# Attention and MLP on one core: softmax denominators of two groups at once on 64x32 tiles, with their inverse rows copied by DMA

## The chip, the cores and the metric

The kernel runs on one core of one Trainium2 chip. Times are device microseconds of one execution. Profiles are of single executions; their span is about 2 us shorter than the time. Engines: PE is TensorE (PEld its weight loads), ACT ScalarE, DVE VectorE, POOL GpSimd, SP SyncE.

## The reference

Eight batches, twelve heads, 448 positions, head dimension 64. q and k are normalized by their root mean square and scaled by a gain per channel; then softmax attention; then an MLP of 768 to 2048 to 768 on all 3584 tokens.

```python
q_n, k_n = rmsnorm(q, g_q), rmsnorm(k, g_k)
attn = softmax(q_n @ k_n.T / 8)            # per batch and head, 448 x 448
x = (attn @ v).transpose(0, 2, 1, 3).reshape(B * S, H * D)
h = x @ w_in
out = (max(h, 0) + alpha * min(h, 0)) @ w_out
```

## The kernel before

Heads go in 24 groups of four. TensorE runs a recorded sequence of bursts: each has two or three score tiles (128 x 896), then perhaps the denominators ("den") or the product with v ("av") of an earlier group, then units of the MLP of an earlier batch: a first-MLP unit ("up", tiles hT or hTa, 6 matmuls) or half a second-MLP unit ("down", tile op, 16 matmuls). Scores, denominators and products use 64x64 tiles of the array, the MLP the whole array.

The denominators are a product of the exponentials with ones, so that each sum comes out on all 64 rows that need it:

```python
def over_keys(name, y, weights):
    acc = psa.tile([128, 2, 512], FP32, name=name, tag="acc")
    ...
    for j in range(J):                     # J = 7
        for g in range(2):
            for par in range(2):           # four 64x64 tiles at once
                nc.tensor.matmul(out=acc[ds(64 * par, 64), g, :S],
                    lhsT=weights(g, par, j), rhs=e[ds(64 * g, 64), j, par, :], ...)

def den(y):
    rden[y] = over_keys("dn", y, lambda g, par, j: ones[ds(64 * g, 64), :])
def log(y):        # ScalarE: Ln out of PSUM
def invert(y):     # ScalarE: Exp(-x), in place; attv multiplies by it on VectorE
```

GpSimd squares q and k and scales them; SyncE transposes them by DMA; VectorE multiplies the transposed k by the gain, in place, fp16 in SBUF:

```python
def square(y, nm):   ...  nc.gpsimd.tensor_mul(out=sqf, in0=src, in1=src)      # sq
def scale(y, nm):    ...  nc.gpsimd.tensor_mul(out=..., in0=nat, in1=rr...)    # qs
def turn(y):
    if y >= TD:                            # groups 8 to 23
        t = qkT[y, "k"]...
        nc.vector.tensor_scalar(out=t, in0=t, scalar1=gain[:, 0:1], ...)       # kT<-kT,gain
        return
```

Every engine works through its own instructions in the recorded order.

## Time and profile before

The median is 453.33 us. The span of the profile is 451.6 us.

| engine | busy us | share of the span |
|---|---|---|
| TensorE | 426.9 | 95% |
| ScalarE | 290.0 | 64% |
| VectorE | 207.8 | 46% |
| GpSimd | 171.2 | 38% |

Average shares mix three stages, so the prediction below reads them stage by stage.

### The profile page before, as it was taken

To read this page: it belongs to the slowest core of one execution; us is meant where nothing else is said; L and a number is where in the kernel's file an instruction comes from. 1 tells how busy PE (TensorE), PEld (TensorE's weight loads), DVE (VectorE), ACT (ScalarE), POOL (GpSimd) and SP (SyncE) were. 2 spreads that over 40 slices of the span, in tenths; PEclk is the share of its full clock that TensorE was granted. 3 is DMA by queue.
4 is the path that set the end of the run, shared out by engine and by line. 5 is a ranking of instruction groups with operands and counts; after the bars stand their busy time and mean duration, and the time that the engine had idled before them with its cause. 6 is when DMAs were issued, how large, how long until landed. Compare 5 with 4: busy or idle time off the path is not lost.

```text
span 451.6 us, 9099 instructions
## 1 busy us (share of the span) xinstructions
PE 426.9 (95%) x3848; PEld 230.0 (51%) x3848; DVE 207.8 (46%) x297; ACT 290.0 (64%) x401; POOL 171.2 (38%) x125
## 2 busy tenths in 40 slices
PE   8768989899999999999999999999999999999996
PEld 3334544555445545455545545455555555455563
DVE  3655553635463544444563544444563343343421
ACT  4998789557875848558785848558785846423300
POOL 5779952751472350750572350750542000000000
PEclk9999999999999999999999999999999999999999
DMA  8999995484655642764664642764361510111122
GB/s 191 233 247 241 232 240 117 60 168 110 158 94 127 159 105 53 140 156 118 157 109 111 158 107 53 139 157 118 77 100 38 77 37 1 37 35 36 35 71 70
DMA packets 60009, 52.77 MB, mean 117 GB/s; under 512 B 32688, under 2 KB 56512, under 8 KB 59968
## 3 DMA queue, kind: packets, MB, share of 16 engines
q1 hardware_dynamic: 47424, 39.27, 36.9%
q0 software_dynamic: 11808, 11.81, 16.7%
q10 hardware_dynamic: 736, 1.11, 1.0%
q8 instruction: 30, 0.49, 0.5%
q14 instruction: 11, 0.09, 0.1%
HBM read 45.62 MB, written 11.01 MB: 125 GB/s over the span
## 4 chain that ended last, share of the span: by engine, by line
PE 79%; ACT 14%; DVE 4%; DMA 1%; issue 1%; SPq 0%; ACTq 0%
PE op L301 31%; PE hT L284 18%; PE hTa L284 9%; ACT expT L229 8%; PE sc L217 7%; PE av L240 5%; PE dn L240 5%; ACT ah L292 2%; PE opa L301 2%; ACT rden L255 2%; DVE gT L293 2%; ACT rden L260 1%; DMA nat<-in_k_dram 1%; PE tps L193 1%; DVE ss L141 1%
## 5 line engine op out<-in xcount | busy, mean ns | idle before, releaser
L229 ACT ACTIVATE expT<-sc,expb 128x896 f16<-128x896 f32 x168 | 157.6, 1008 | 18.9 <-PE sc L217 18.7
L301 PE MATMUL op<-w_out_sb,gT 128*128 128x384 f16 x848 | 145.9, 326 | 2.1 <-DVE gT L293 2.0
L158 POOL TENSOR_TENSOR qs<-nat,rr 128x896 f16<-128x896 f32 x44 | 78.3, 1799 | 177.7 <-issue 159.0
L284 PE MATMUL hT<-xT,w_in_sb 128*128 128x448 f16 x558 | 117.1, 353 | 2.7 <-DVE gT L293 2.6
L301 PEld LDWEIGHTS <-gT 128*128 128x128 f16 x896 | 84.6, 98 | 65.5 <-issue 12.3
L284 PEld LDWEIGHTS <-w_in_sb 128*128 128x128 f16 x768 | 73.7, 98 | 72.8 <-issue 8.5
L292 ACT ACTIVATE ah<-hT,cols 128x448 f16<-128x448 f32 x93 | 59.1, 636 | 59.5 <-PE hT L284 59.4
L293 DVE TENSOR_TENSOR gT<-hT,ah 128x448 f16<-128x448 f32 x93 | 58.0, 624 | 76.5 <-ACT ah L292 76.5
L135 POOL TENSOR_TENSOR sq<-nat 128x896 f32<-128x896 f32 x44 | 73.0, 1681 | 1.4 <-DMA nat<-in_q_dram 1.3
L313 DVE COPY osb<-op 128x384 f32<-128x384 f32 x53 | 29.5, 557 | 89.4 <-PE op L301 89.4
L217 PE MATMUL sc<-qT,kT 64*64 64x448 f16 x672 | 53.2, 359 | 9.5 <-ACT expT L229 6.0
L292 ACT ACTIVATE ah<-hTa,cols 128x448 f16<-128x448 f32 x35 | 22.2, 633 | 49.5 <-PE hTa L284 49.5
L141 DVE TENSOR_REDUCE ss<-sq 128x14 f32<-128x896 f32 x48 | 49.8, 1076 | 6.5 <-ACT sq L133 6.1
L284 PE MATMUL hTa<-xT,w_in_sb 128*128 128x448 f16 x210 | 45.4, 352 | 0.0
L217 PEld LDWEIGHTS <-kT 64*64 64x64 f16 x672 | 19.2, 104 | 39.1 <-issue 29.0
L240 PE MATMUL av<-expT,vt 64*64 64x448 f16 x672 | 36.0, 350 | 2.2 <-ACT rden L255 2.2
L293 DVE TENSOR_TENSOR gT<-hTa,ah 128x448 f16<-128x448 f32 x35 | 21.8, 623 | 31.3 <-ACT ah L292 31.3
L240 PE MATMUL dn<-expT,ones 64*64 64x448 f16 x672 | 35.9, 349 | 0.2 <-DVE gT L293 0.2
L268 DVE TENSOR_TENSOR xT<-av,rden 128x896 f16<-128x896 f32 x24 | 26.2, 1090 | 20.7 <-PE av L240 20.7
L240 PEld LDWEIGHTS <-vt 64*64 64x64 f16 x672 | 20.3, 107 | 14.3 <-issue 3.7
L240 PEld LDWEIGHTS <-ones 64*64 64x64 f16 x672 | 20.5, 107 | 11.9 <-issue 1.0
L260 ACT ACTIVATE rden<-rden 128x896 f32<-128x896 f32 x24 | 23.0, 957 | 0.6
(37 smaller groups left out, 134.0 us busy)
## 6 DMA issues: line engine op xcount, KB each, us to landing
out_dram<-osb SPq DMA_DIRECT2D x54, 192.0 KB, 2.7
nat<-in_q_dram SPq DMA_DIRECT2D x46, 224.0 KB, 6.1
nat<-in_k_dram SPq DMA_DIRECT2D x46, 224.0 KB, 6.9
vt<-in_v_dram POOLq DMA_DIRECT2D x16, 336.0 KB, 7.6
w_in_sb<-in_moe_w_in_dram POOLq DMA_DIRECT2D x4, 768.0 KB, 13.2
w_out_sb<-in_moe_w_out_dram POOLq DMA_DIRECT2D x4, 768.0 KB, 16.6
nat<-in_q_dram ACTq DMA_DIRECT2D x2, 224.0 KB, 4.6
nat<-in_k_dram ACTq DMA_DIRECT2D x2, 224.0 KB, 6.1
```

Of the source, the lines that this page charges most:

```text
L135: nc.gpsimd.tensor_mul(out=sqf, in0=src, in1=src)
L141: nc.vector.tensor_reduce(out=ss_t[y][:, "qk".index(nm)].rearrange("p h j -> p (h j)").unsqueeze(2), in_=sqs[y, nm], axis=AXIS_X, op=ALU.add,)
L158: eng.tensor_mul(out=t.rearrange("p j h d -> p h j d"), in0=nat[y, nm], in1=rr_t[y][:, "qk".index(nm)].unsqueeze(3).broadcast_to((128, 2, ...
L217: nc.tensor.matmul(out=sc[ds(64 * g, 64), par, :S].rearrange("p (j c) -> p j c", j=J), lhsT=kT[ds(64 * par, 64), j, g, :], rhs=qT[ds(64 * ...
L229: nc.scalar.activation(out=expT[y][:, j], in_=scs[y, j][:, :, :S], func=AF.Exp, scale=QK_SCALE, bias=expb[:, 0:1],)
L240: nc.tensor.matmul(out=acc[ds(64 * par, 64), g, :S], lhsT=weights(g, par, j), rhs=e[ds(64 * g, 64), j, par, :], start=(j == 0), stop=(j == ...
L260: nc.scalar.activation(out=r, in_=r, func=AF.Exp, scale=-1.0)
L284: nc.tensor.matmul(out=hT[:, :S], lhsT=w_in_sb[:, c, ts(ft, 128)], rhs=x[:, c, :], start=(c == order[0]), stop=(c == order[-1]),)
L292: nc.scalar.activation(out=ah, in_=hT[:, :S], func=AF.Copy, scale=alpha_sb[:, ft : ft + 1])
L293: nc.vector.tensor_max(out=gT[:, ft, ds((b & 1) * S, S)], in0=hT[:, :S], in1=ah)
L301: nc.tensor.matmul(out=op[:, :OH], lhsT=gT[:, ft, ts(t, 128)], rhs=w_out_sb[:, ft, ds(oh * OH, OH)], start=(ft == 0), stop=(ft == NF - 1),)
L313: nc.vector.tensor_copy(out=o[:, ds(oh * OH, OH)], in_=op[:, :OH])
```

## The change

From group 6 on the denominators of two groups are computed together. A 64x32 tile puts each sum on 32 rows only, so eight tiles run side by side in place of four. One Ln then serves two groups, and the Exp is written twice. Each inverse then has the right values in two bands of 32 rows and the other group's in the other two, which a DMA within SBUF overwrites. The rest makes room for that: a third buffer for the exponentials, "down" units kept for bursts with den or av, row sums a burst sooner, av two or three bursts behind its den. To fit, the squares have three buffers where they had four, and ah two where it had three.

```diff
+    def den(ys):
+        if len(ys) == 1: ...              # as before, groups 0 to 5
+        dn = psa.tile([128, 2, 512], FP32, name="dn2", tag="acc")
+        for j in range(J):
+            for par in range(2):
+                for n, y in enumerate(ys):
+                    for g in range(2):
+                        nc.tensor.matmul(
+                            out=dn[ds(64 * par + 32 * n, 32), g, :S],
+                            lhsT=ones[ds(64 * g, 64), :32],
+                            rhs=expT[y][ds(64 * g, 64), j, par, :], ...)
...
+        for y in ys:
+            nc.scalar.activation(out=rden[y], in_=r, func=AF.Exp, scale=-1.0)
+        if len(ys) == 2:
+            for n, y in enumerate(ys):
+                for c in range(2):
+                    nc.gpsimd.dma_start(
+                        out=rden[y][ds(64 * c + 32 * (1 - n), 32)],
+                        in_=rden[y][ds(64 * c + 32 * n, 32)],
+                    )
...
-                if old and (free or not ups):
+                if old and (not ups or free and (
+                    wide(n) or len(old) > sum(wide(c) for c in range(n, hi))
+                )):
...                                        # bursts, jobs, turns and spare banks
```

More of the change, by code (lines that the diff above doesn't have):

```diff
@@ L49 @@
     TD = min(8, NG)
+    PD = min(6, NG)
+    EB = 3
     cst = ctx.enter_context(tc.tile_pool(name="cst", bufs=1))
@@ L129, in square @@
         src = nat[y, nm].rearrange("p h j d -> p (h j d)")
-        sq = ld.tile([128, 2 * J, D], FP32, name="sq", tag="sq", bufs=4)
+        sq = ld.tile([128, 2 * J, D], FP32, name="sq", tag="sq", bufs=3)
         sqf = sq.rearrange("p n d -> p (n d)")
@@ L227, in soft @@
         if j == 0:
-            expT[y] = att.tile([128, J, 2, S], FP16, name="expT", tag="expT")
+            expT[y] = att.tile([128, J, 2, S], FP16, name="expT", tag="expT", bufs=EB)
         nc.scalar.activation(
@@ L247, in over_keys, with log, invert @@
         return acc
-    def den(y):
-        dn = over_keys("dn", y, lambda g, par, j: ones[ds(64 * g, 64), :])
-        rden[y] = dn
-    def log(y):
-        r = att.tile([128, 2, S], FP32, name="rden", tag="rden")
-        nc.scalar.activation(out=r, in_=rden[y][:, :, :S], func=AF.Ln)
-        rden[y] = r
-    def invert(y):
-        r = rden[y]
-        nc.scalar.activation(out=r, in_=r, func=AF.Exp, scale=-1.0)
+    def den(ys):
+        if len(ys) == 1:
+            rden[ys[0]] = over_keys(
+                "dn", ys[0], lambda g, par, j: ones[ds(64 * g, 64), :]
+            )
+            return
+        dn = psa.tile([128, 2, 512], FP32, name="dn2", tag="acc")
[6 more added lines that the diff above has]
+                            lhsT=ones[ds(64 * g, 64), :32],
+                            rhs=expT[y][ds(64 * g, 64), j, par, :],
+                            start=(j == 0),
+                            stop=(j == J - 1),
+                        )
+        for y in ys:
+            rden[y] = dn
+    def log(ys):
+        r = att.tile([128, 2, S], FP32, name="rden", tag="rden")
+        nc.scalar.activation(out=r, in_=rden[ys[-1]][:, :, :S], func=AF.Ln)
+        rden[ys[-1]] = r
+    def invert(ys):
+        r = rden[ys[-1]]
+        for y in ys[:-1]:
+            rden[y] = att.tile([128, 2, S], FP32, name="rden", tag="rden")
+        for y in ys:
+            nc.scalar.activation(out=rden[y], in_=r, func=AF.Exp, scale=-1.0)
[5 more added lines that the diff above has]
+                        in_=rden[y][ds(64 * c + 32 * n, 32)],
+                    )
     def attv(y):
@@ L290, in up @@
             )
-        ah = ffn.tile([128, S], FP16, name="ah", tag="ah", bufs=3)
+        ah = ffn.tile([128, S], FP16, name="ah", tag="ah", bufs=2)
         nc.scalar.activation(out=ah, in_=hT[:, :S], func=AF.Copy, scale=alpha_sb[:, ft : ft + 1])
@@ L335 @@
     bursts, dens, avs, first_in, last_in = [], {}, {}, {}, {}
+    den_at, av_at = {}, {}
     m = 0
     while m < NG * J or len(avs) < NG:
-        n = len(bursts)
-        if len(dens) > len(avs):
-            avs[n] = len(avs)
-        elif len(dens) < NG and last_in.get(len(dens), n) < n:
-            dens[n] = len(dens)
-        wide = n in dens and dens[n] >= G or n in avs and avs[n] >= G
-        count = min(3 if wide else 2, NG * J - m)
-        bursts.append([divmod(m + c, J) for c in range(count)])
-        for y, j in bursts[n]:
-            first_in.setdefault(y, n)
+        n, y, d = len(bursts), len(avs), len(den_at)
+        if y in den_at and n - den_at[y] >= (2 if y >= PD else 1):
+            avs[n] = y
+            av_at[y] = n
+        elif d < NG:
+            ys = [d] if d < PD else [d, d + 1]
+            if all(last_in.get(g, n) < n for g in ys):
+                dens[n] = ys
+                den_at.update((g, n) for g in ys)
+        three = n in dens and dens[n][0] >= G or n in avs and avs[n] >= G
+        tiles = []
+        while len(tiles) < (3 if three else 2) and m < NG * J:
+            g, j = divmod(m, J)
+            if j == 0 and g >= EB and not (
+                g - EB in av_at and (av_at[g - EB] < n or len(tiles) == 2)
+            ):
+                break
+            tiles.append((g, j))
+            first_in.setdefault(g, n)
             if j == J - 1:
-                last_in[y] = n
-        m += count
+                last_in[g] = n
+            m += 1
+        bursts.append(tiles)
     NB = len(bursts)
-    den_at = {y: n for n, y in dens.items()}
-    av_at = {y: n for n, y in avs.items()}
     prep, post, roots = {}, {}, {}
@@ L366 @@
     turns = {n: y for y, n in turn_at.items()}
-    jobs = {}
-    for y in range(G, NG):
-        early = y < G + 2
-        n = turn_at[y - 1] if early else max(d for d in dens if d <= turn_at[y] - 2)
-        at(n - (8 if early else 5), load_qk, y)
-        for nm in "qk":
-            (after if early else at)(n - 2, square, y, nm)
-            if early:
-                after(n, reduce, y, nm)
-            else:
-                jobs.setdefault(n, []).append((reduce, (y, nm)))
-        roots[n + 1] = y
-    for b in range(1, B):
-        at(av_at[G * b] - 4, load_v, b)
     UP, DOWN = 1.13, 2.6
@@ L402, in cost, with wide @@
         )
+    def wide(n):
+        return n in dens or n in avs
     first = av_at[G - 1]
+    begin = [av_at[G * b + G - 1] for b in range(B)]
+    for b in range(3, B - 1, 2):
+        begin[b] = max(begin[b], (begin[b - 1] + begin[b + 1]) // 2)
     gaps = [[] for _ in range(NB)]
     for b in range(B - 1):
-        lo, hi = av_at[G * b + G - 1], av_at[G * b + 2 * G - 1]
+        lo, hi = begin[b], begin[b + 1]
         ups, old, new = (list(u) for u in periods[b])
@@ L435 @@
     rest += [u[1:] for u in old + new]
+    jobs = {}
+    for y in range(G, NG):
+        early = y < G + 2
+        n = turn_at[y - 1] if early else turn_at[y] - 4
+        if not early:
+            for c in (4, 5, 3):
+                if turn_at[y] - c not in jobs and any(
+                    u[0] is down for u in gaps[turn_at[y] - c]
+                ):
+                    n = turn_at[y] - c
+                    break
+            while n in jobs:
+                n -= 1
+        at(n - (8 if early else 5), load_qk, y)
+        for nm in "qk":
+            (after if early else at)(n - 2, square, y, nm)
+            if early:
+                after(n, reduce, y, nm)
+            else:
+                jobs.setdefault(n, []).append((reduce, (y, nm)))
+        roots.setdefault(n + 1, []).append(y)
+    for b in range(1, B):
+        at(av_at[G * b] - 4, load_v, b)
     load_qk(0)
@@ L481 @@
         at(first - 2 + c, load_w_out, c)
-    roots[4] = 2
+    roots.setdefault(4, []).append(2)
     for n in range(NB):
@@ L507 @@
             attv(avs[n])
+        pair = n in dens and len(dens[n]) == 2
+        if pair:
+            log(dens[n])
         for t in tiles[2:]:
@@ L513 @@
             late = [(1, soft, t) for t in tiles[1:]]
-        if n in roots:
-            y = roots[n]
+        for y in roots.get(n, ()):
             root(y)
@@ L520 @@
                 turn_dma(y)
-        if n in dens and not lead:
+        if n in dens and not lead and not pair:
             log(dens[n])
@@ L526 @@
                 late = [(1, invert, (dens[n],))]
+        elif pair:
+            if gaps[n] and gaps[n][0][0] is down:
+                invert(dens[n])
+            else:
+                late = [(2, invert, (dens[n],))]
         done = 0
-        spare_at, clock = None, 0.0
+        spare_at, clock = [], 0.0
         for k, (f, a) in enumerate(gaps[n][:-1]):
             free = 2.3 if n in dens else 1.2 if n in avs else 0.1
-            if spare_at is None and clock >= free and not turns.get(n, TD) < TD:
-                spare_at = k
+            if clock >= free and not turns.get(n, TD) < TD and (
+                not spare_at or k - spare_at[-1] > 2
+            ):
+                spare_at.append(k)
             clock += DOWN if f is down else UP
         for k, (f, a) in enumerate(gaps[n]):
-            spare = k == spare_at
+            spare = k in spare_at
             if f is down:
@@ L545 @@
                     late = []
-            if k == 0 and n in turns:
+            if n in turns and k == (
+                0 if turns[n] >= TD else max(min(1, len(gaps[n]) - 2), 0)
+            ):
                 turn(turns[n])
@@ L551 @@
             g(*c)
-        if n < first and plain and n not in turns:
+        if n < den_at[G - 1] - 1 and plain and n not in turns:
             spin(4)
```

## The prediction

> **What bounds the kernel now.** I read first the windows view, cut where the chain of work changes hands (columns: length, then busy us of PE, PE weight loads, DVE, ACT, POOL, each with its instruction count, then clock, DMA share, GB/s).
>
> ```profile
> 0.00:92.00 92.00, 76.45 (x813) 39.51 (x814) 48.82 (x65) 72.90 (x101) 63.05 (x55) 1.00 0.96 198
> 92.00:375.00 283.00, 278.70 (x2558) 150.45 (x2556) 133.53 (x192) 196.77 (x273) 108.12 (x70) 1.00 0.52 111
> 375.00:451.60 76.60, 71.71 (x481) 40.06 (x478) 25.45 (x41) 20.29 (x30) 0.00 (x0) 0.99 0.16 42
> ```
>
> From 92 to 375 us TensorE works 278.70 of 283.00 us at full clock; every other engine has over 80 us free. Before 92 us ScalarE (72.90) rivals TensorE, and the last stretch is MLP work alone with a drain of the output. What TensorE still waits for after 92 us is little, by the view of waits cut to that stretch:
>
> ```profile
> PE hT L284 <- DVE gT L293: 2.4, 5, 0.9
> PE op L301 <- DVE gT L293: 2.0, 2, 1.0
> PE dn L240 <- DVE gT L293: 0.2, 1, 0.2
> ```
>
> So there a microsecond of TensorE work removed is a microsecond of time, if no new wait comes. I then read what one denominator costs, in the chain of work (start, us, what):
>
> ```profile
> 204.24 0.50 PE sc L217 x8
> 204.75 1.32 PE dn L240 x28
> 206.07 0.19 PE sc L217 x4
> 206.26 2.71 PE op L301 x16
> ```
>
> The single instructions behind this show four dn matmuls (four 64x64 tiles) starting 3.3 ns apart, and the next four 189 ns after the first: 7 steps of 189 ns = 1.32 us per group, 24 groups.
>
> They also show what a change of tile shape costs. Eight score matmuls followed by dn or av in the same shape take 0.402 us, by op or hT 0.505; six hT before scores take 1.228 us, before another unit 1.135; the first score step is 24 ns longer, the first op step behind scores 10. One visit to 64x64 and back is thus 0.103 + 0.093 + 0.024 + 0.010 = 0.23 us.
>
> ScalarE's rows, which decide where it may become the bound:
>
> ```profile
> L229 ACT ACTIVATE expT<-sc,expb 128x896 f16<-128x896 f32 x168 | 157.6, 1008 | 18.9 <-PE sc L217 18.7
> L292 ACT ACTIVATE ah<-hT,cols 128x448 f16<-128x448 f32 x93 | 59.1, 636 | 59.5 <-PE hT L284 59.4
> L260 ACT ACTIVATE rden<-rden 128x896 f32<-128x896 f32 x24 | 23.0, 957 | 0.6
> L255 ACT ACTIVATE rden<-dn 128x896 f32<-128x896 f32 x24 | 22.3, 929 | 1.3 <-PE dn L240 1.3
> ```
>
> **What the Trainium skill says.** "TensorEngine Tiling (Array Packing)", Tiling Modes, lists 64x32 as eight independent tiles, and says that changing the mode drains the engine. The trace agrees on the drain (the 0.23 us a visit); it has no 64x32 tile. "TensorE: Matmul & The Clock Gate", Part 3, gives concurrent tiles a span of one matmul plus about 4 ns per further tile, up to 16 tiles; the trace agrees for four (3.3 ns). "ScalarE: Activation LUTs", What ACT_TABLE_LOAD costs, prices an ACTIVATE by elements per lane, not by partitions; so one Ln over four 32-row bands costs what it costs today. The 0.93 us of 128x896 fits. "DMA: Bandwidth & Descriptors", Anatomy of one DMA, gives a fixed cost near 2 us; here small transfers land in 2.7 us (out_dram<-osb) to 3.4 (kT<-qs, a transpose).
>
> **The change part by part.** I took the order of instructions of both kernels and counted.
>
> 1. Denominators. Groups 6 to 23 (18 groups) go in 9 pairs of 56 matmuls. With all eight tiles at once a step is 189 + 4 x 3.3 = 202 ns at worst, more likely 189 with 13 ns once, so a pair takes about 1.34 us. Saved: 18 x 1.323 - 9 x 1.34 = 23.8 - 12.1 = 11.7 us of TensorE, all after 96 us, on the path.
>
> 2. Tile-shape changes. Bursts grow from 66 to 77, as a pair's two av come two and three bursts behind its den, and waiting for two groups makes bursts without den or av. Visits out of 128x128 go from 61 to 70: 9 x 0.23 = 2.1 us. A pair also changes 64x64 to 64x32 and back, 16 changes in the order; half a visit (0.115) each is my estimate: 1.8 us. Matmul counts of all other kinds are equal but for one idle filler of four in the opening.
> Net TensorE work: -11.7 + 2.1 + 1.8 = -7.8 us.
>
> 3. ScalarE. A pair needs one Ln and two Exp instead of two and two: 9 x 0.929 = 8.4 us less. It isn't the bound in the large stretch (196.77 of 283), so this buys nothing there by itself.
>
> 4. New waits on ScalarE by rearrangement. With den 6 put off to be paired with 7, bursts 21 to 24 hold two score tiles and 1, 2, 3, 3 first-MLP units, where the old burst 21 had a second-MLP unit (2.6 us of TensorE with no ScalarE work). Sums for bursts 19 to 26, from the rows above plus 0.55 us for each root (0.33 + 0.23): ScalarE 4.9 + 3.7 + 3.2 + 3.3 + 4.5 + 3.9 + 5.9 + 3.8 = 33.2 us. TensorE, with 1.13 us a unit, 2.6 a second-MLP unit, 0.6 a plain score visit: 2.1 + 6.6 + 1.7 + 2.9 + 4.0 + 4.0 + 5.0 + 2.9 = 29.2. A plain burst with two first-MLP units also puts its second exp behind the first unit's ah, so the next burst's second score tile waits some 0.5 us (score tiles have two buffers). I follow it burst by burst and get waits of 1.85, 0.3, 0.3, 1.0, 0.5, 0.55 us in bursts 21 to 31: 4.5 us. The old kernel loses 1.8 between 96 and 133 us (0.09, 0.86, 0.07, 0.77), which putting second-MLP units behind den is made to remove. Net +2.7. From burst 31 on, bursts have four or five units or a second-MLP unit, and TensorE's sum is larger again. The 1.0 us waits of op behind the last unit of a sequence (189 and 291 us) stay: the order is the same there.
>
> 5. The opening. Turning group 4 behind two units rather than one removes most of the 1.1 us wait at 64.6 us; dropping a filler of four brings 0.2 at most, as the Ln behind it also waits for the root before it (ends 41.22, Ln starts 41.43). Taken: -1.2.
>
> 6. The copies. 36 of 115 KB (32 x 896 x 4 bytes), 4.1 MB beside 52.8. GpSimd issues one in 0.5 to 0.7 us (rows 0.50, vt 0.68): 18 to 25 us more on an engine that works 108 of 283. Is a pair's inverse there in time? From the end of the denominators: Exp of both ready at about 3.7 and 4.7 us (first two exps, Ln, third exp, Exp, Exp), two issues 1.2 us, landing 3 us: 7.9 us for the first group. Its av ends, by the order, 0.3 + 2.6 + 0.6 + 2.3 + 0.4 + 1.3 = 7.5 us on for the first pair, 7.8 for the second, 10 to 11 for the others; and behind that av stands a second-MLP unit of 2.6 us that needs neither the product nor VectorE until its end. So nearly all is hidden. GpSimd waiting in order for the Exp delays the next squares and scales by some 6 us; for group 10 I find kT ready at about 22.0 us against its first score at 22.3. I allow 1 us for copies and turns together. Earlier row sums are there to make this fit.
>
> Sum: -7.8 + 2.7 - 1.2 + 1.0 = -5.3, and about -0.4 for other waits that the shorter bursts behind den lose: 453.3 - 5.7 = 447.6 us.
>
> **The rivals.**
> A. The eight tiles don't run at once: two moving streams per row of the array are shown in this trace, four aren't. Then a pair takes 2.65 us, nothing is saved, and the switches and waits stay: 453.3 + 3.9 + 1.5 = about 459. Against it: the skill's table of packed tiles. I give it 12%.
> B. The change of column width costs little (weights of seven tiles are loaded while the last streams), and the rearrangement removes the ScalarE waits rather than moving them: -11.7 + 2.1 + 0.5 - 1.8 - 1.2 = -12, about 441. For it: parts of the change look like answers to just such waits. Against: bursts 21 to 26 have more ScalarE work than TensorE work. 20%.
> C. The inverse copies are late (landing 6 us as the q and k loads, 6.1 and 6.9, when they share the 16 engines): VectorE then stands in order behind xT, gT comes late, the MLP banks fill. Two tight pairs would lose 2 to 3 us each, and delayed turns 1 us on each of several groups: 452 to 455. Against it: DMA share is 0.52 in that stretch. 10%.
>
> **Range and chances.** The remaining 58% lie within 2.5 us of 447.6. With the rivals' places, 8 in 10 is 442.0 to 455.0. Faster by over 2% means under 444.3, 3.3 us below my sum, which rival B and the edge of the middle give: 0.24. Slower by over 2% means over 462.4, past even rival A: 0.04. Within: 0.72.
>
> **What would show it.** The steps in turn: (1) eight dn2 matmuls starting within 30 ns and the next eight 190 to 200 ns later, a pair near 1.34 us in the chain; (2) the gap between scores and dn2 near 0.1 us; (3) half of the Ln gone from burst 25 on; (4) TensorE waiting for expT between 96 and 130 us, some 4 us in sum, and next to nothing later; (6) xT waiting for a rden copy at most at the first two pairs, copies landing in about 3 us. A dn2 step near 380 ns makes the prediction wrong by rival A; xT or kT waits for DMA throughout by rival C; no ScalarE waits in 96 to 130 us by rival B.

## More of the kernel before

One more view matters for what came, that of the instructions that write kT. Its columns are the shortest, median and longest duration in ns, then first and last start in us.

```profile
L179 DVE TENSOR_SCALAR kT<-kT,gain x16: 445/658/975, 112.9 to 362.9; 128x896 f16<-128x896 f16 x16
```

Sixteen products of kT with the gain take 0.45 to 0.98 us.

## The result

The changed kernel takes 463.48 us (463.47 to 464.16, four runs) against 453.6: the ratio is 1.0222, with a 95% interval of 1.0204 to 1.024, so slower. A ratio here is the mean time of one kernel's fast runs over that of the other's of the same rounds, so it is not quite the ratio of the medians.

The windows view of the changed kernel, with columns as in the prediction and the middle cut once more:

```profile
0.00:92.00 92.00, 76.07 (x802) 38.88 (x803) 45.92 (x63) 71.99 (x100) 60.04 (x52) 0.98 0.94 195
92.00:135.00 43.00, 36.01 (x327) 17.35 (x326) 24.41 (x28) 28.52 (x42) 21.68 (x17) 0.92 0.60 120
135.00:386.00 251.00, 241.47 (x2271) 122.28 (x2268) 122.91 (x167) 163.00 (x227) 104.26 (x88) 0.99 0.57 120
386.00:461.70 75.70, 71.05 (x450) 39.65 (x449) 25.48 (x41) 17.41 (x26) 1.97 (x4) 0.99 0.19 48
```

TensorE now idles 7.0 of 43 us right behind the opening and 9.5 of 251 after that, and its clock there is 0.92 and 0.99 where it was 1.00.

First, did the tiles do what they were to do? The timeline of TensorE around a pair (start, us, engine, line, what):

```profile
309.02 0.57 PE L219 MATMUL sc<-qT,kT 64*64 64x448 f16 x8
309.53 1.52 PE L263 MATMUL dn<-expT,ones 64*32 64x448 f16 x56
310.97 0.38 PE L219 MATMUL sc<-qT,kT 64*64 64x448 f16 x4
```

They did. From 309.53 to 310.97 it is 1.44 us for two groups, where one took 1.32. By the single instructions, eight matmuls start within 24 ns, the next eight 199 ns after the first, and the steps after that are 189 ns apart.

Then the waits of TensorE after 92 us (what waited, for what: us in total, times, longest):

```profile
PE hT L315 <- DVE gT L324: 6.2, 4, 5.2
PE sc L219 <- DVE kT L181: 5.9, 5, 3.8
PE sc L219 <- ACT expT L231: 3.5, 6, 1.4
```

The third line was predicted. The first two hold one wait of 5.2 us and one of 3.8, and these are new. The chain of work through the second one (start, us, what):

```profile
121.37 5.81 DVE kT L181
127.18 0.04 issue
127.22 0.59 PE sc L219 x4
127.81 5.23 PE op L332 x16
133.04 0.50 PE sc L219 x8
```

An instruction that took at most 0.98 us takes 5.81, and 16 op matmuls behind it take 5.23 us instead of 2.60. The view of kT's product, to be held against the row of the kernel before:

```profile
L181 DVE TENSOR_SCALAR kT<-kT,gain x16: 444/887/5798, 112.0 to 363.7; 128x896 f16<-128x896 f16 x16
```

What else ran then? The timeline of VectorE and of GpSimd in the same stretch:

```profile
121.37 5.80 DVE L181 TENSOR_SCALAR kT<-kT,gain 128x896 f16<-128x896 f16 x1
127.09 0.61 DVE L324 TENSOR_TENSOR gT<-hT,ah 128x448 f16<-128x448 f32 x1
```
```profile
118.23 2.06 POOL L288 DMA_DIRECT2D rden<-rden  x4 [5.83 <-ACT rden L283]
120.31 3.33 POOL L137 TENSOR_TENSOR sq<-nat 128x896 f32<-128x896 f32 x2
123.58 3.33 POOL L160 TENSOR_TENSOR qs<-nat,rr 128x896 f16<-128x896 f32 x2
```

GpSimd stood 5.83 us at the copies, for ScalarE's Exp. Released, it issued them and then ran two squares and two scales without a gap, from 120.31 to 126.91. VectorE's product began within that row and ended 0.26 us behind it. The same happens at 317.55 (5.80 us, again behind two squares and two scales); there gT stands behind it on VectorE and TensorE waits the 5.2 us.

Four findings make up the loss. The stall at 127 us costs 3.8 us and then 2.6 in which op runs at half speed; that at 324 us costs 5.2 and 1.3 (six hT matmuls in 2.40 us instead of 1.14): 12.9 us together. ("TensorE: Matmul & The Clock Gate", Part 1 of the Trainium skill, has the clock halve after an idle window of about 3.4 us. The window agrees, as the half-clock stretches of these traces, but for those cut off by their ends, last 3.41 or 6.83 us. But TensorE need not idle through all of it: it worked 0.80 us of the 3.42 us before the first halving and none before the second, and in before_useless_copies below a pause of 1.56 us was enough, with 1.70 us of work in the 3.41 us before.) A copy that landed late adds 1.3 and 0.7 at 159 to 161 us, and three smaller kT waits 1.4. That is some 16 us; the run without copies below keeps 2.2 us of kT waits, so about 14 of them would be the copies'.

My theory (called L in the expectations): a product on VectorE can't run while GpSimd works through a row of its own instructions, and the copies on GpSimd's queue put such a row where the product is due. The Trainium skill, "SBUF — State Buffer", Who interferes with whom, describes the first half: VectorE's `tensor_scalar` may use two ports, of which one pair is shared with GpSimd and lent to one of them exclusively. I hadn't looked that page up. In the same trace VectorE's other work is not held: all 128 gT products take 0.61 to 0.63 us, 53 of them while GpSimd works. No run here gave the product a form that leaves the shared ports alone, so that it is the ports rests on the page and on this timing. The rival (S): the new order of bursts itself is at fault, kT comes too late or VectorE is overfilled, and the copies are bystanders.

### The profile page after: what moved, and what is told of

Same layout as the page of the kernel before. It is cut to its first block, busy times and chain, and to the rows that moved or that the text cites. A ratio compares the mean times of both kernels' runs of the same rounds, so it can differ in the third digit from the quotient of the medians.

```text
span 461.7 us, 9170 instructions
## 1 busy us (share of the span) xinstructions
PE 424.6 (92%) x3844; PEld 218.2 (47%) x3844; DVE 218.7 (47%) x297; ACT 280.9 (61%) x392; POOL 188.0 (41%) x161
## 4 chain that ended last, share of the span: by engine, by line
PE 68%; ACT 17%; DVE 9%; DMA 3%; issue 2%; SPq 0%; POOL 0%; DVEq 0%; ACTq 0%
PE op L332 28%; PE hT L315 18%; ACT expT L231 9%; PE hTa L315 7%; PE sc L219 7%; PE av L242 5%; DVE kT L181 3%; ACT rden L283 3%; ACT ah L323 2%; PE opa L332 2%; DMA rden<-rden 2%; ACT rden L275 2%; DVE gT L324 2%; PE dn L263 2%; DVE ss L143 2%
## 5 line engine op out<-in xcount | busy, mean ns | idle before, releaser
L231 ACT ACTIVATE expT<-sc,expb 128x896 f16<-128x896 f32 x168 | 161.4, 1006 | 34.9 <-PE sc L219 34.7
L332 PE MATMUL op<-w_out_sb,gT 128*128 128x384 f16 x848 | 148.4, 330 | 0.0
L315 PE MATMUL hT<-xT,w_in_sb 128*128 128x448 f16 x588 | 124.5, 355 | 7.7 <-DVE gT L324 6.4
L323 ACT ACTIVATE ah<-hT,cols 128x448 f16<-128x448 f32 x98 | 62.1, 633 | 86.2 <-PE hT L315 80.8
L324 DVE TENSOR_TENSOR gT<-hT,ah 128x448 f16<-128x448 f32 x98 | 61.2, 624 | 82.5 <-ACT ah L323 82.2
L288 POOL DMA_DIRECT2D rden<-rden x36 | 18.3, 515 | 89.9 <-ACT rden L283 89.8
L315 PE MATMUL hTa<-xT,w_in_sb 128*128 128x448 f16 x180 | 38.9, 352 | 0.0
L323 ACT ACTIVATE ah<-hTa,cols 128x448 f16<-128x448 f32 x30 | 19.1, 636 | 24.9 <-PE hTa L315 24.9
L324 DVE TENSOR_TENSOR gT<-hTa,ah 128x448 f16<-128x448 f32 x30 | 18.7, 623 | 21.9 <-ACT ah L323 21.9
L181 DVE TENSOR_SCALAR kT<-kT,gain 128x896 f16<-128x896 f16 x16 | 22.1, 1380 | 0.0
```

The costliest lines, as they stand in the source:

```text
L231: nc.scalar.activation(out=expT[y][:, j], in_=scs[y, j][:, :, :S], func=AF.Exp, scale=QK_SCALE, bias=expb[:, 0:1],)
L315: nc.tensor.matmul(out=hT[:, :S], lhsT=w_in_sb[:, c, ts(ft, 128)], rhs=x[:, c, :], start=(c == order[0]), stop=(c == order[-1]),)
L323: nc.scalar.activation(out=ah, in_=hT[:, :S], func=AF.Copy, scale=alpha_sb[:, ft : ft + 1])
L324: nc.vector.tensor_max(out=gT[:, ft, ds((b & 1) * S, S)], in0=hT[:, :S], in1=ah)
L332: nc.tensor.matmul(out=op[:, :OH], lhsT=gT[:, ft, ts(t, 128)], rhs=w_out_sb[:, ft, ds(oh * OH, OH)], start=(ft == 0), stop=(ft == NF - 1),)
```

## The experiments

Each is one edit of the kernel that its expectation names, except sync_gain_pool, which changes the engine and the place of the product together. Ratios are to the kernel before in the same rounds, whose medians were 453.6 to 454.2 us.

**No copies.** The result is wrong (its relative error is 0.96).

```diff
-        if len(ys) == 2:
+        if False:
```

> The changed kernel without the 36 copies; the result is wrong on purpose. Theory L with its cause in GpSimd's order: 445 to 449 us, the time that the change would have without the copies' side effects, ScalarE waits of TensorE of some 6 us between 96 and 145 us left. Rival S: 456 to 463 us, as only the one xT wait (2 us) goes.

449.04 us, ratio 0.9889 (0.9856 to 0.9922). The waits of TensorE after 92 us:

```profile
PE sc L219 <- ACT expT L231: 3.5, 6, 1.4
PE sc L219 <- DVE kT L181: 2.2, 2, 1.4
PE hT L315 <- DVE gT L324: 1.3, 4, 0.4
```

Without 36 small DMAs the order of bursts is all the same, and 14.4 us are gone. S falls. The 3.5 us for expT are the price of the new order (I had expected some 6), and the longest kT product here is 2.24 us.

**Only the copies, in the kernel before.** The reverse: nothing of the change except useless copies by GpSimd.

```diff
         nc.scalar.activation(out=r, in_=r, func=AF.Exp, scale=-1.0)
+        if y >= 6 and y % 2:
+            for c in range(4):
+                nc.gpsimd.dma_start(
+                    out=spare_rows[ds(32 * c, 32)], in_=r[ds(32 * (c ^ 1), 32)])
```

> The kernel before plus, behind each odd group's inverse from group 7 on, four copies of 32 rows issued by GpSimd into a tile that nobody reads: only GpSimd's standing still at the Exp and its four issues are added. Theory L with its cause in GpSimd's order: squares are held back and reach kT's products in some bursts, at least one kT product over 3 us, 455 to 466 us. Rival (it takes the new order of bursts too): every kT product under 1.7 us, 453 to 454.5 us.

462.24 us, ratio 1.018 (1.0163 to 1.0197): clear of noise. The result is correct. The timelines of VectorE and GpSimd at the worst product:

```profile
227.69 4.94 DVE L180 TENSOR_SCALAR kT<-kT,gain 128x896 f16<-128x896 f16 x1
```
```profile
223.87 0.50 POOL L264 DMA_DIRECT2D spare_rows<-rden  x1
224.38 3.33 POOL L136 TENSOR_TENSOR sq<-nat 128x896 f32<-128x896 f32 x2
227.66 3.33 POOL L159 TENSOR_TENSOR qs<-nat,rr 128x896 f16<-128x896 f32 x2
230.93 1.36 POOL L111 DMA_DIRECT2D vt<-in_v_dram  x2
```

In the kernel before, at this place:

```profile
227.88 0.97 DVE L179 TENSOR_SCALAR kT<-kT,gain 128x896 f16<-128x896 f16 x1
```
```profile
226.91 3.48 POOL L158 TENSOR_TENSOR qs<-nat,rr 128x896 f16<-128x896 f32 x2 [6.09 <-DMA out_dram<-osb]
```

The product came while GpSimd was in its first scale and got in behind it. The useless copies hold the squares back to 224.38, and the product meets squares, scales and two DMA issues in one row: 4.94 us. A second one takes 3.55. The copies alone thus bring 8 us of loss to the old order: TensorE waits 4.5 us for these two products, and behind each its clock is halved for 3.41 us.

**Copies issued by SyncE.**

```diff
-                    nc.gpsimd.dma_start(
+                    nc.sync.dma_start(
                         out=rden[y][ds(64 * c + 32 * (1 - n), 32)],
```

> The changed kernel with the 36 copies issued by SyncE instead of GpSimd. Theory L with its cause in GpSimd's order (its queue stands at the copies until the Exp, so squares that used to run ahead start just when kT's product is due): squares run ahead again, no kT product over 1.7 us, and no copy stands behind a load of v; 446 to 450 us. Rival S: nothing changes for kT, 458 to 465 us. A third way: SyncE now stands at the Exp and loads and turns come late, 452 to 460 us with waits for nat or kT.

450.16 us, ratio 0.991 (0.9876 to 0.9943), correct. The longest kT product is 2.25 us, over the 1.7 that I gave, and TensorE still waits 3.1 us for kT. The third way did not come: SyncE's standing still cost nothing visible. The DMA rows of the changed kernel and of this one (KB each, median us to landing):

```profile
rden<-rden POOLq DMA_DIRECT2D x36, 112.0 KB, 3.2
```
```profile
rden<-rden SPq DMA_DIRECT2D x36, 112.0 KB, 2.2
```

In the changed kernel the four copies at 150 us took 7.2 to 7.8 us; two loads of v had been issued on the same queue 3.6 and 2.9 us earlier, and the copies landed after both. SyncE's slowest took 4.7. That the copies stood behind the loads of v is not shown: in the next run copies of 9.9 to 10.1 us landed over 5 us after the last load of v before them.

**Squares behind scales.** Copies stay on GpSimd; the squares of a burst are recorded at its end.

```diff
-            (after if early else at)(n - 2, square, y, nm)
+            after(n - 2, square, y, nm)
```

> The changed kernel with the squares of a burst recorded at its end, so behind the scales, copies left on GpSimd. If only a row that begins with squares holds VectorE (in all rows that begin with scales so far kT's product got in between the two scales): no kT product over 1.7 us, 448 to 453 us. If any unbroken row of four holds it: kT products of 5 us and more remain, 457 to 465 us. Rival S: 458 to 465 us.

452.86 us, ratio 0.9976 (0.9935 to 1.0017). No kT product is over 1.58 us, as in the first branch. What is left over no_copies is one late copy at 151 us (VectorE stands 7.0 us at xT for it, TensorE 3.6). But sync_turn_early, below, shows that the order of squares and scales was not the point, and the second branch doesn't hold either: at 112 and 122 us the product got into an unbroken row of two scales and two squares.

**kT's product a burst sooner**, with the copies on GpSimd, and again with them on SyncE.

```diff
+    turns = {n - (y >= TD): y for n, y in turns.items()}
```

> The changed kernel, copies left on GpSimd, with kT's product from group 8 on one burst sooner. Theory L says that where the product meets GpSimd's row matters, not that it is there: if it now comes before the held-back squares start, 449 to 453 us, no product over 2 us; if it meets a row all the same, gT stands behind it and it stays at 455 us or more, even though the scores have a burst more to spare.

474.62 us, ratio 1.0442 (1.0404 to 1.0479): the worst of all, by the second branch. VectorE and GpSimd at one of three such places:

```profile
220.02 7.42 DVE L181 TENSOR_SCALAR kT<-kT,gain 128x896 f16<-128x896 f16 x1
```
```profile
218.94 3.34 POOL L137 TENSOR_TENSOR sq<-nat 128x896 f32<-128x896 f32 x2
222.21 3.34 POOL L160 TENSOR_TENSOR qs<-nat,rr 128x896 f16<-128x896 f32 x2
225.50 1.69 POOL L137 TENSOR_TENSOR sq<-nat 128x896 f32<-128x896 f32 x1
```

Five GpSimd instructions without a gap, and the product ends 0.26 us behind the fifth. The scores had a burst more to spare, and it helped nothing: the gT products stand behind it on VectorE, and the MLP and av wait for those (12.0 us before av alone).

> copies_by_sync (450.2 us) with kT's product from group 8 on recorded one burst sooner; TensorE's order is the same. There the transposed kT lies ready 4 to 16 us before its product, and the score matmuls still wait 3.1 us in sum for products that stand behind GpSimd. If only the place is too late: these 3.1 us go, 446.5 to 449 us. If the waits move to gT, as VectorE stands all the same: 449 to 451.

453.19 us, ratio 0.9975 (0.9933 to 1.0016): slower than copies_by_sync, outside both ranges. (By the trace of copies_by_sync kT lies ready 6 to 14 us before its product, not 4 to 16.) I had expected waits only to move; instead the first product now began at 109.09, with GpSimd in the second of two DMA issues for v, and stood through this, two scales and a square: 5.61 us. So it isn't only squares that hold it, and that no product was held for long in squares_behind_scales may have been luck of the moment.

**kT's product on another engine.** First on ScalarE, with the copies on GpSimd.

```diff
-            nc.vector.tensor_scalar(out=t, in0=t, scalar1=gain[:, 0:1], ...)
+            nc.scalar.activation(out=t, in_=t, func=AF.Copy, scale=gain[:, 0:1])
```

> The changed kernel with the product of kT and the gain on ScalarE instead of VectorE. Theory L (VectorE's fp16 product stands behind a row of GpSimd instructions, twice for 5.80 us, and the two stalls of 6.6 us each of TensorE with its halved clock come of it): both stalls and the smaller kT waits (0.77, 0.74, 0.34, 0.32 us) go, ScalarE has 16 instructions of about 1 us more; 448 to 452 us, clock back at 1.00 after 92 us. Rival S (the stalls come of the new order itself: kT transposed too late, or VectorE simply over-filled): kT is as late as before, 458 to 465 us.

453.49 us, ratio 0.9986 (0.9949 to 1.0023). Both long stalls are gone, which is what L says of its first half, but my 448 to 452 missed: the 16 products of 1.04 us put up to 1.6 us of waits on hT for gT, 3.9 us in sum, and the scores still wait 1.5 us for kT, now from ScalarE.

> copies_by_sync (450.2 us) with kT's product on ScalarE, so that VectorE has nothing left that stands behind GpSimd. The score matmuls wait 3.1 us for kT there; ScalarE gets 16 instructions of 1.04 us, which in gain_on_scalar put some 2 us of new waits on gT and hT. If the standing behind GpSimd was the larger: 447.5 to 449.5 us; if the load on ScalarE is: 450 to 453.

453.08 us, ratio 0.9987 (0.9973 to 1.0002), at the upper end of the second range: with ScalarE doing the products it makes no difference who issues the copies, and the load on ScalarE is larger than the standing that it removes.

> copies_by_sync with kT's product on GpSimd itself, a burst sooner, where it waits in one queue with squares and scales and cannot be held by them out of turn. GpSimd gets 16 instructions of perhaps 1 to 2 us and has 150 us free. If the product is always in time: 446.5 to 449 us; if GpSimd, in order, brings the product or the scales behind it late: 450 to 456.

449.98 us, ratio 0.9918 (0.99 to 0.9935), between the two ranges. GpSimd takes 2.5 us for a product, one wait of 2.0 us remains for the first of them.

**The other parts of the change.** First without the pairs (`PD = NG`), so every other part stays and there is nothing to copy.

> The changed kernel with every denominator by itself, so without 64x32 tiles and without copies; all other parts of the change (placing of second-MLP units, third expT buffer, earlier row sums, turns) stay. If the loss sits in the pairs and their copies: 449 to 454 us, near the kernel before, no kT product over 1.7 us, waits of TensorE after 92 us no more than the 4.6 us of before. If the other parts carry some of it: 456 us or more.

453.2 us, ratio 0.9978 (0.9961 to 0.9994), in the first range. Two of its signs failed: the longest kT product takes 1.89 us, and the waits come to 5.1 us. The other parts are worth 1 us. Pairs without copies' side effects are worth 4 more (449.04, in another round).

Then, on copies_by_sync, the old rule for "down" units (the last minus and plus of the diff above undone), and groups 6 and 7 taken singly (`PD = 8`).

> copies_by_sync (450.2 us) with the old rule for the place of second-MLP units: one first in every burst while there are any, not kept for the bursts with denominators or products. The plain bursts near 98 to 110 us then hold a second-MLP unit alone, so the 3.5 us that TensorE waits there for expT should go; in return first-MLP units stand behind den and av and wait for ScalarE's Ln and Exp, as in the kernel before (0.8 us each time). If the placing is worth its name, 451 to 455 us; if it costs more than it brings, 446 to 449.5.

456.18 us, ratio 1.0047 (1.0024 to 1.0071): worse than I gave it. The waits for expT did not go (3.4 us) and kT products behind GpSimd came back (4.9 us). The placing is worth its name in this schedule, though part of it is where it puts the products of kT.

> copies_by_sync with groups 6 and 7 by themselves and 8 pairs instead of 9. One pair's saving of 1.2 us is lost (2 x 1.32 less 1.45), the bursts around 98 us get denominators and second-MLP units again, where TensorE now waits 1.7 + 0.5 + 1.3 us for expT: if these waits come from pairing too early, 447 to 449.5 us; if they only move, 450.5 to 453.

450.26 us, ratio 0.9914 (0.9899 to 0.9928): between the two ranges, and the same as with nine pairs. TensorE's waits for expT are 4.1 us in place of 3.5, so they moved, and one pair's 1.2 us were paid back by shorter waits for kT (1.4 us in place of 3.1).

The best correct kernels, copies_by_sync, sync_eight_single and sync_gain_pool, take 0.8 to 0.9% less than the kernel before, and 3% less than the changed one.

## Why the prediction was wrong

**Step 1, the tiles: right.** 1.448 us from the first matmul of a pair to the next score is 1.33 of work and 0.11 of tile change. Rival A is refuted.

**Step 2, tile changes: right in size.** Eight score matmuls ahead of a pair take 0.503 us, ahead of 64x64 work 0.402: a change from 64x64 to 64x32 costs 0.10, like one to 128x128 (0.103). The trace has the 70 visits and the 16 changes that were counted.

**Step 3, ScalarE: right.** Nine Ln fewer; the Ln row fell from 22.3 to 13.8 us.

**Step 4, new waits for ScalarE: right in kind, a little large.** 3.5 us of waits for expT, where I had worked out 4.5; they lie at 92 to 145 us. The two 1.0 us waits of op that I let stay are gone: in no_copies no op waits, and the longest wait for gT is 0.43 us.

**Step 5, the opening: wrong, but small.** The wait of 1.1 us in front of the transposes is still there (64.84 us), released as before by VectorE's xT.

**Step 6 failed: "I allow 1 us for copies and turns together".** The copies cost 14.4 us, and the turns 2.2 us of waits for kT even without them. The prediction had the cause in hand ("GpSimd waiting in order for the Exp delays the next squares and scales by some 6 us") and then asked only whether what GpSimd makes would be in time. It was in time: in the changed kernel the transposed kT lies ready 3.3 to 14.8 us before its product. What I left out is what the delayed row would meet. In the kernel before, GpSimd runs ahead: the squares are done long before, and only two scales are near kT's product, which gets in behind the first. Held at the copies, GpSimd runs squares and scales in one row, and VectorE stands until the row ends. Since VectorE goes in order, gT stands too, then TensorE, and after such a pause TensorE's clock is halved for some microseconds. Rival C named late copies and late turns; the one late copy that came, at the second pair, cost 2.0 us, and no turn waited for its transpose. None of the rivals had the wait that took the place.

One more thing holds the squares back, which I overlooked: with three buffers for them in place of four, GpSimd also waits for VectorE's row sums (43.0 us after 92 us in the changed kernel, 54.6 in no_copies, none in the kernel before). It isn't what cost the 14.4 us, as no_copies has it too, and before_useless_copies shows the loss without it. Whether the kT waits that remain come of it is open; no run had four buffers.

The rest of the sum comes near: my estimate without the 1 us for step 6 is 446.6 us, no_copies measured 449.0. That it comes so near is partly luck: the 2.2 us of waits for kT and the 1.1 us of step 5 make it longer, the 1.0 us too much in step 4 and the op waits that went make it shorter.

## What to carry to other kernels

When an in-order engine is given a wait, ask not only whether its results still come in time, but what its later work will now run beside. A duration that varies for one instruction on one shape (0.45 to 0.98 us here) can be a wait in disguise, as it was here; find out for what before moving anything near it. If a helper DMA needs a queue, choose one whose engine has no work that must run ahead: here SyncE instead of GpSimd turned 463.5 us into 450.2.

## What the Trainium skill lacked or had wrong

- "SBUF — State Buffer", Who interferes with whom: the page says that whoever issues first has the pair for the whole instruction and the other blocks. It does block, but not only for one instruction: VectorE's product stood behind up to five GpSimd instructions in a row (7.42 us, 0.44 undisturbed), while others got in between two instructions (0.46 to 1.64 us). What decides between the two is open. Products that first met a square, a scale (4.59 us at 301 us in sync_old_free) or a DMA issue were each held. A start 0.26 us before the end of a GpSimd instruction was held in after_turn_early (150 us) and let in in no_pairs (161 us); likewise, a start 0.62 us before it was held in the changed kernel (121 us), and one 0.58 us before it was let in in squares_behind_scales (112 us).
- The same page: DMA issues by GpSimd in such a row don't let VectorE in either; 5.61 us from within an issue through two scales and a square, and 4.94 us through two scales and then two issues. But an issue alone need not hold it: four products of after_turn_early began 0.2 us into an issue of a copy and took 0.44 us.
- "TensorE: Matmul & The Clock Gate", Part 1: the window before a halving need not be idle. TensorE had worked 1.39 us of the 3.41 us before the one at 116.5 us in sync_gain_pool, and 1.90 before the one at 38.9 us in no_pairs. Between 1.42 and 1.90 us it went either way in these traces; no stretch with more work was followed by one.
- "TensorEngine Tiling (Array Packing)", Key Properties: says that changing the mode drains the engine, without a cost. Here it is about 0.10 us a change, for 64x64 to 64x32 as to 128x128. Eight 64x32 tiles with eight different moving operands run at once in steps of 189 ns, as four 64x64 tiles do, which no table of the page shows for this shape.
